# Decode attention over two caches: the TensorE program of the second part as a loop over chunk pairs, with fixed buffer pairs

## The chip, the cores and the metric

The kernel runs on one core of a Trainium2 chip. The metric is the device time of one execution in microseconds (us), as the median of several runs. The profiled span, from the first to the last instruction, is about 1.8 us shorter than the measured time.

TensorE is called PE here, and PEld is its weight load, which has its own row in the profile. DVE is VectorE, ACT is ScalarE, POOL is GpSimd, and SP is the engine that issues the large transfers. T, S and PV are the three matmul groups of a chunk: transposing K, scores, and probabilities times V.

## The reference

There are two attention layers with one query token each, whose outputs are concatenated. Layer A has 8 key/value heads for 32 query heads and sees only the last 2048 positions. Layer B has 32 heads and sees all 8192. The batch is 4 and the head size 128.

```python
# A: W = min(4096, max(256, Sk // 4)), only the last W positions, each kv head serves 4 query heads
# B: all Sk = 8192 positions, H = 32
q = (x @ wq).reshape(B, Sq, H, Dh).transpose(0, 2, 1, 3)
scores = jnp.einsum("bhqd,bhkd->bhqk", q, k_cache) * (Dh ** -0.5)
p = softmax(scores, axis=-1)
o = jnp.einsum("bhqk,bhkd->bhqd", p, v_cache)
out = o.transpose(0, 2, 1, 3).reshape(B, Sq, H * Dh) @ wo      # [...] concatenated: A, then B
```

The caches of B alone are 2 x 268 MB, so the kernel mostly reads memory.

## The kernel before

The work is cut into chunks: 8 of A (one key/value head, all batches, 2 MB of K and 2 MB of V) and 64 of B (two heads of one batch, 4 MB and 4 MB). K and V land in ten "halves" of 2 MB each, which are dealt out as a ring:

```python
def take(load, n, release, at=None):
    if at is None:
        if n == 2 and ring[0] % 2:
            ring[0] += 1
        at = ring[0] % NH            # NH = 10 halves; an A load takes one, a B load two
        ring[0] = at + n
    waits = []
    for i in range(at, at + n):
        waits += held[i]             # the last reader of the half: T for a K, PV for a V
        held[i] = [release]
    half_of[load] = at
    return at, waits
```

The loads go out on one queue in the order K(c+1), V(c), with the last four V at the end. A chunk has 16 groups of 8 tiles (8 in A). PE transposes a group of K (T), another engine copies it out of PSUM, and PE multiplies it with the query (S). After softmax, PE multiplies with V (PV). A table by group index mixes T, S and PV of several chunks, and the whole list is written out:

```python
for s in range(len(groups)):
    when(s, 0, lambda s=s: emit_T(s))
    when(s + SLAG, 2, lambda s=s: emit_S(s))
# [...] statistics
    v0 = max(s0 + PVLAG[ch["ab"]], v_end)            # PVLAG = {0: 6, 1: 8}
    for g in range(ch["NG"]):
        when(v0 + g, 4, lambda c=c, g=g: emit_pv(c, g))
# [...]
@block.tensor
def _(e):
    sch.emit("pe", e, sems)          # 26704 matmuls, each with its weight load, no loop
```

Of the kernel before, what the change touches and what calls it, by code (L numbers as in the profile page):

```python
# [12 lines left out]
P = 128  # L13
# [5 lines left out]
NPB = {0: 2, 1: 4}  # L19
NSM = 4  # L20
SLAG = 2
NW = 64
PVLAG = {0: 6, 1: 8}
# [5 lines left out]
class _Sched:  # L29


    def __init__(self):
        self.tk = {}
        self.ops = {n: [] for n in ("sp", "pe", "dve", "act", "pool")}
        self.count = {n: 0 for n in self.ops}
        self.dma_uses = {}

    def add(self, eng, emit, waits=(), key=None):
        sig = None
        if key is not None:  # L40
            self.count[eng] += 1
            sig = ("eng_" + eng, 1)
            assert key not in self.tk, key
            self.tk[key] = ("eng_" + eng, self.count[eng])
        self.ops[eng].append((emit, tuple(waits), sig))

    def add_dma(self, eng, emit, semname, waits=(), key=None):
        n = self.dma_uses.get(semname, 0) + 1
        self.dma_uses[semname] = n
        if key is not None:  # L50
            assert key not in self.tk, key
            self.tk[key] = (semname, 16 * n)
        self.ops[eng].append((emit, tuple(waits), (semname, 16)))

    def emit(self, engname, eng, sems):
        waited = {}
        for emit, waits, sig in self.ops[engname]:
            need = {}
            for w in waits:
                sname, val = self.tk[w]  # L60
                if need.get(sname, 0) < val:
                    need[sname] = val
            for sname, val in need.items():
                if waited.get(sname, 0) >= val:
                    continue
                eng.wait_ge(sems[sname], val)
                waited[sname] = val
            ins = emit(eng)
            if sig is not None:
                ins.then_inc(sems[sig[0]], sig[1])  # L70


def bass_concat_heads__sliding_block_cached__mha_block_cached__decode_kernel(
# [49 lines left out]

    sch = _Sched()
    with ExitStack() as es:
# [9 lines left out]
        kt = sb("kt", [P, NKT, TG * P], BF16)  # L135
        wor = sb("wor", [P, NWO, 4 * DO], BF16)
# [17 lines left out]
        rst = {0: sb("rsa", [P, NSM, 16], F32), 1: sb("rsb", [P, NSM, 2 * NB], F32)}  # L154
        rinv = sb("rinv", [P, NSM, 16], F32)
        pbt = {0: sb("pba", [P, NPB[0], NTA * 16 + NW], BF16), 1: sb("pbb", [P, NPB[1], NTB * 2 + NW], BF16)}
        oT = sb("oT", [P, NSM, 16], BF16)
        outsb = sb("outsb", [36, DO], BF16)
# [22 lines left out]
        sch.add("pool", lambda e: e.memset(rst[1][:, :, :], 0.0), key="c_rs")  # L181
# [6 lines left out]
        ring = [0]  # L188

        def take(load, n, release, at=None):  # L190
            if at is None:
                if n == 2 and ring[0] % 2:
                    ring[0] += 1
                at = ring[0] % NH
                ring[0] = at + n
# [5 lines left out]
            return at, waits  # L201
# [7 lines left out]
        def dma_wq(ab, at):  # L209

            at, waits = take(("wq", ab), 2, ("qmm", ab), at)
# [3 lines left out]
        def dma_wo(i):  # L215
# [4 lines left out]
            waits = [("fin", wo_last[i - NWO])] if i >= NWO else []  # L220
            sch.add_dma("sp", lambda e: e.dma_start(dst, src), "d_wo%d" % slot, waits=waits, key=("wo", i))

        def dma_kv(kind, c):
            ch = chunks[c]
            T = {("k", 0): A_k, ("k", 1): B_k, ("v", 0): A_v, ("v", 1): B_v}[(kind, ch["ab"])]
            at, waits = take((kind, c), 1 if ch["ab"] == 0 else 2, ("T", ch["s_last"]) if kind == "k" else ("pv", c))
# [18 lines left out]
        dma_wq(0, NH - 2)  # L245
        dma_kv("k", 0)
        dma_wq(1, NH - 4)

        loads = [("k", c + 1) for c in range(NC - 1)]
        for c in range(NC):  # L250
            loads.insert(2 * c + 1 if c < NC - 4 else len(loads), ("v", c))
# [12 lines left out]
        rs_read = [[] for _ in range(NSM)]  # L264


        def emit_xT():
            for ab in (0, 1):
                xv = xs[:, ab, :].rearrange("b (p r) -> b r p", r=KC)
                for r in range(KC):  # L270
                    o = xtps[:, (ab * KC + r) * NB:(ab * KC + r + 1) * NB]
                    i_ = xv[:, r, :]
                    sch.add("pe", lambda e, o=o, i_=i_: e.transpose(o, i_, identb[0:NB, 0:NB]),
                            waits=[("x", 0), ("x", 1), "c_identb"], key="xTmm" if (ab == 1 and r == KC - 1) else None)
# [4 lines left out]
        def emit_q(ab):  # L279
            wqr = flat(half_of[("wq", ab)], 2)  # L280
            for h in range(HQ):
                for r in range(KC):
                    o = ms[:, Q0 + h * NB: Q0 + (h + 1) * NB]
                    l = wqr[:, (r * HQ + h) * P:(r * HQ + h + 1) * P]
                    rr = xT[:, ab, r * NB:(r + 1) * NB]
                    last = h == HQ - 1 and r == KC - 1
                    sch.add("pe", lambda e, o=o, l=l, rr=rr, r=r: e.matmul(o, l, rr, start=(r == 0), stop=(r == KC - 1)),
                            waits=[("wq", ab), "xT"] + ms_read if h == r == 0 else [],
                            key=("qmm", ab) if last else None)
# [18 lines left out]

        def emit_T(s):
            c, g = groups[s]  # L310
            bank = s % NTRB
            for t in range(TG):
                o = tr[:, bank, t * P:(t + 1) * P]
                i_ = tile_of("k", c, g * TG + t)
                waits = []
                if t == 0:
                    waits = [("k", c), "c_identb"] + ([("ev", s - NTRB)] if s >= NTRB else [])
                sch.add("pe", lambda e, o=o, i_=i_: e.transpose(o, i_, identb[:, :]),  # L318
                        waits=waits, key=("T", s) if t == TG - 1 else None)
            src, dst = tr[:, bank, :], kt[:, s % NKT, :]  # L320
            waits = [("T", s)] + ([("S", s - NKT)] if s >= NKT else [])
            if s % 3 == 2 or (c < NCA and s % 2 == 1):
# [7 lines left out]

        def emit_S(s):
            c, g = groups[s]
            ch = chunks[c]
            for t in range(TG):
                j = g * TG + t
                if ch["ab"] == 1:
                    bank, o0, col = c % 2, 2 * j, NB * HQ + ch["b"] * HQ + 2 * ch["hp"]
                else:
                    bank, o0, col = j // HT, 16 * (j % HT), 16 * ch["g"]

                n = min(NW, 512 - o0)
                q = qs[:, col:col + n]
                o = sc[:, bank, o0:o0 + n]
                l = kt[:, s % NKT, t * P:(t + 1) * P]
                waits = []
                if t == 0:
                    waits = [("ev", s), ("q", ch["ab"])] + sc_read[bank]
                    sc_read[bank] = []
                sch.add("pe", lambda e, o=o, l=l, q=q: e.matmul(o, l, q, start=True, stop=True),  # L349
                        waits=waits, key=("S", s) if t == TG - 1 else None)  # L350
# [35 lines left out]
        def stats_gmax(c):  # L386
# [3 lines left out]
            sch.add("pe", lambda e: e.transpose(ms[0:C, col:col + P], rm[:, m, 0:C], identf[:, :]),  # L390
                    waits=[("rowmax", c), "c_identf"] + ms_read, key=("trm", c))
# [10 lines left out]
        def stats_exp(c):  # L402
# [3 lines left out]
            sch.add("pe", lambda e: e.matmul(ms[:, col:col + C], gx[0:C, m, :], identf[0:C, 0:C], start=True, stop=True),  # L406
                    waits=[("gx", c)] + ms_read, key=("bc", c))
            sch.add("dve", lambda e: e.tensor_copy(negb[:, m, 0:C], ms[:, col:col + C]), waits=[("bc", c)], key=("negb", c))  # L408
            ms_read[:] = [("negb", c)]
            i = c % NPB[ab]  # L410
            prev = c - NPB[ab]
            pw = [("c_pb", ab)] + ([("pv", prev)] if prev >= (0 if ab == 0 else NCA) else [])
            pbv = pbt[ab][:, i, 0:ch["NT"] * ch["UC"]].rearrange("p (j x) -> p j x", x=ch["UC"])
            r = ch["norm"] % NSM
            if ab == 1:
                for u, pp in HALVES:
                    src = sc[pp, c % 2, 0:NTB * 2].rearrange("p (j u) -> p u j", u=2)[:, u, :]
                    ri = rst[1][pp, r, ch["n0"] + u:ch["n0"] + u + 1]
                    sch.add("act", lambda e, src=src, pp=pp, ri=ri, u=u: e.activation(  # L419
                        pbv[pp, :, u], src, ACTF.Exp, bias=negb[pp, m, 0:1], scale=scale, accum_out=ri),  # L420
                        waits=[("negb", c), "c_rs"] + rs_read[r] + pw, key=("exp", c) if u == 1 else None)
# [14 lines left out]
            sch.add("dve", lambda e: e.tensor_reduce(out=rs4[:, r, :], in_=ev.rearrange("p (j c) -> p c j", c=C), axis=AX.X, op=ALU.add),  # L436
                    waits=[("exp1", c)], key=("rs4", c))
            sch.add("dve", lambda e: e.tensor_tensor(  # L438
                out=rst[0][:, r, :].rearrange("p (b c) -> p b c", b=NB), in0=bcast(rs4[:, r, :], [[0, NB], [1, C]]),
                in1=bcast(mk[:, :], [[1, NB], [0, C]]), op=ALU.mult),  # L440
                waits=[("rs4", c)] + rs_read[r], key=("rs", c))


        def emit_pv(c, g):
            ch = chunks[c]
            UC = ch["UC"]
            base = (ch["norm"] % NSM) * 16 + ch["n0"]
            for t in range(TG):
                j = g * TG + t
                n = NW if c < NC - 4 else UC  # L450
                o = po[:, base:base + n]
                l = tile_of("v", c, j)
                r = pbt[ch["ab"]][:, c % NPB[ch["ab"]], j * UC:j * UC + n]
# [3 lines left out]
                elif j == 0:  # L457
                    waits += [("v", c)]
                sch.add("pe", lambda e, o=o, l=l, r=r, j=j: e.matmul(o, l, r, start=(j == 0), stop=(j == ch["NT"] - 1)),  # L459
                        waits=waits, key=("pv", c) if j == ch["NT"] - 1 else None)  # L460

        def norm_n(c):
            return chunks[c]["norm"] % NSM, 16 if chunks[c]["ab"] == 0 else 2 * NB

        def norm_sum(c):
            m, n = norm_n(c)
            sch.add("pe", lambda e: e.matmul(ms[:, L0:L0 + n], onesf[:, :], rst[chunks[c]["ab"]][:, m, 0:n], start=True, stop=True),
                    waits=[("rs", c), "c_onesf"] + ms_read, key=("L", c))
            sch.add("dve", lambda e: e.reciprocal(out=rinv[:, m, 0:n], in_=ms[:, L0:L0 + n]), waits=[("L", c)], key=("rinv", c))
# [3 lines left out]
        def norm_out(c):  # L473
            m, n = norm_n(c)
            sch.add("dve", lambda e: e.tensor_tensor(out=oT[:, m, 0:n], in0=po[:, m * 16:m * 16 + n], in1=rinv[:, m, 0:n], op=ALU.mult),  # L475
                    waits=[("rinv", c), ("pv", c)], key=("oT", c))
            po_read[:] = [("oT", c)]

        def emit_fin(c):
            ch = chunks[c]  # L480
            ab = ch["ab"]
            m, n = norm_n(c)
            w = wor[:, ch["wo"] % NWO, :].rearrange("p (hl n) -> p hl n", hl=4)
            p0 = 0 if ab == 1 else 32
            if ab == 1:
                ov = oT[:, m, 0:n].rearrange("p (b u) -> p b u", u=2)
                ops = [(ov[:, :, u], w[:, (2 * ch["hp"] + u) % 4, :]) for u in range(2)]
            else:
                ov = oT[:, m, 0:n].rearrange("p (u c) -> p u c", c=REP)
# [100 lines left out]
```

## Time and profile before

| | before |
|---|---|
| time, median of 4 runs | 1419.8 us (1419.24 to 1420.34) |
| profiled span, granted PE clock | 1417.6 us, 0.958 |
| data queue q1 | 587.22 MB, 97.8% |
| instruction transfers of PE (fetches, queue q8) | 208, 1.0% |
| PE waits called "issue" (PE rows) | 41.4 + 33.8 + 33.4 = 108.6 us |

PE's rows of the waits say what PE lacks; the columns are total us, times, longest.

```profile
PE tr L318 <- DMA kv<-in_B_k_cache_dram: 96.5, 51, 4.5
PE po L459 <- issue: 41.4, 44, 2.4
PE sc L349 <- issue: 33.8, 32, 2.6
PE tr L318 <- issue: 33.4, 34, 2.2
```

PE lacks K for 96.5 us, and it lacks something that is no data for 108.6 us, in many short pieces.

### The profile page before, as it was taken

To read this page: it belongs to the slowest core of one execution; us is meant where nothing else is said; L and a number is where in the kernel's file an instruction comes from. 1 tells how busy PE (TensorE), PEld (TensorE's weight loads), DVE (VectorE), ACT (ScalarE), POOL (GpSimd) and SP (SyncE) were. 2 spreads that over 40 slices of the span, in tenths; PEclk is the share of its full clock that TensorE was granted. 3 is DMA by queue.
4 is the path that set the end of the run, shared out by engine and by line. 5 is a ranking of instruction groups with operands and counts; after the bars stand their busy time and mean duration, and the time that the engine had idled before them with its cause. 6 is when DMAs were issued, how large, how long until landed. Compare 5 with 4: busy or idle time off the path is not lost.

```text
span 1417.6 us, 55508 instructions
## 1 busy us (share of the span) xinstructions
PE 1148.0 (81%) x26704; PEld 1088.8 (77%) x26704; DVE 618.3 (44%) x1167; ACT 454.4 (32%) x649; POOL 19.6 (1%) x20
## 2 busy tenths in 40 slices
PE   4778888878888888887878888888787788888887
PEld 4667787778777778887778778877777788778786
DVE  1766443444444444444434444444344334434452
ACT  1443333323233333232333223333233233323331
POOL 1111000000000000000000000000000000000000
PEclk8999999999999999999999999999999999999997
DMA  9999999999999999999999999999999999999994
GB/s 400 414 417 422 429 426 429 429 426 430 427 427 426 426 427 432 416 424 429 411 429 426 419 404 431 417 426 415 418 428 427 423 412 416 429 422 408 423 426 206
DMA packets 30159, 590.76 MB, mean 417 GB/s; under 512 B 2656, under 2 KB 10864, under 8 KB 11120
## 3 DMA queue, kind: packets, MB, share of 16 engines
q1 hardware_dynamic: 29912, 587.22, 97.8%
q8 instruction: 208, 3.41, 1.0%
q14 instruction: 15, 0.12, 0.0%
q10 hardware_dynamic: 24, 0.01, 0.0%
HBM read 587.21 MB, written 0.01 MB: 414 GB/s over the span
## 4 chain that ended last, share of the span: by engine, by line
DMA 59%; PE 31%; DVE 6%; issue 3%; ACT 0%; SPq 0%; DVEq 0%
DMA kv<-in_B_k_cache_dram 57%; PE tr L318 14%; PE po L459 7%; PE sc L349 7%; DMA kv<-in_A_k_cache_dram 2%; DVE kt L325 2%; DVE sA L368 1%; PE ms L406 1%; DVE rsa L438 1%; PE fin L495 1%; DVE rm L383 1%; PE ms L390 1%; DVE sel L361 1%; DVE rm L378 0%; DVE rs L436 0%
## 5 line engine op out<-in xcount | busy, mean ns | idle before, releaser
L318 PE MATMUL tr<-identb,kv 128*128 128x128 bf16 x8704 | 690.7, 223 | 132.7 <-DMA kv<-in_B_k_cache_dram 96.5
L325 DVE COPY kt<-tr 128x1024 bf16<-128x1024 bf16 x704 | 486.6, 691 | 683.7 <-PE tr L318 680.8
L323 ACT ACTIVATE kt<-tr 128x1024 bf16<-128x1024 bf16 x384 | 392.3, 1024 | 854.8 <-PE tr L318 851.0
L318 PEld LDWEIGHTS tr<-identb,kv 128*128 128x128 bf16 x8704 | 520.0, 100 | 145.1 <-DMA kv<-in_B_k_cache_dram 103.0
L349 PE MATMUL sc<-qs,kt 128*128 128x64 bf16 x8704 | 449.8, 195 | 39.1 <-issue 33.8
L459 PE MATMUL po<-pbb,kv 128*128 128x64 bf16 (+1 forms) x8192 | 413.1, 192 | 43.5 <-issue 41.4
L349 PEld LDWEIGHTS sc<-qs,kt 128*128 128x128 bf16 x8704 | 373.2, 99 | 45.0 <-issue 35.9
L459 PEld LDWEIGHTS po<-pbb,kv 128*128 128x128 bf16 x8192 | 316.2, 99 | 56.8 <-issue 53.6
L419 ACT ACTIVATE pbb<-sc,negb 64x128 bf16<-64x128 f32 x128 | 51.5, 402 | 81.7 <-DVE negb L408 80.4
L383 DVE TENSOR_REDUCE rm<-sc 64x1 f32<-64x128 f32 x128 | 36.5, 285 | 18.5 <-PE sc L349 17.6
L390 PE MATMUL ms<-identf,rm 128*1 128x128 f32 (+1 forms) x72 | 21.0, 291 | 25.3 <-DVE rm L378 14.3
L390 PEld LDWEIGHTS ms<-identf,rm 128*1 128x1 f32 (+1 forms) x72 | 6.2, 86 | 35.1 <-DVE rm L383 19.2
L406 PEld LDWEIGHTS ms<-identf,gx 1*128 1x128 f32 (+1 forms) x144 | 21.1, 182 | 11.7 <-DVE gx L399 6.0
L406 PE MATMUL ms<-identf,gx 1*128 1x1 f32 (+1 forms) x144 | 27.2, 256 | 2.3 <-DVE gx L399 1.6
L459 PE MATMUL po<-pba,kv 128*128 128x64 bf16 x512 | 25.4, 193 | 0.0
L395 DVE TENSOR_REDUCE gm<-ms 1x2 f32<-1x128 f32 (+1 forms) x72 | 19.6, 272 | 11.6 <-PE ms L390 11.6
L495 PE MATMUL fin<-wor,oT 128*4 128x512 bf16 x64 | 18.3, 386 | 7.0 <-DVE oT L475 7.0
L419 ACT ACTIVATION_READ_ACCUMULATOR pbb<-sc,negb 64x1 f32 x128 | 23.7, 185 | 0.0
L459 PEld LDWEIGHTS po<-pba,kv 128*128 128x128 bf16 x512 | 19.1, 98 | 3.1 <-issue 3.1
L408 DVE COPY negb<-ms 128x1 f32<-128x1 f32 (+1 forms) x72 | 11.0, 152 | 15.4 <-PE ms L406 15.4
L368 DVE TENSOR_REDUCE sA<-sel 128x128 f32<-128x512 f32 x16 | 16.9, 1059 | 0.5
L399 DVE TENSOR_SCALAR gx<-gm 1x128 f32<-1x128 f32 (+1 forms) x72 | 15.9, 221 | 2.5
(36 smaller groups left out, 106.8 us busy)
## 6 DMA issues: line engine op xcount, KB each, us to landing
kv<-in_B_k_cache_dram SPq DMA_DIRECT2D x64, 4096.0 KB, 29.6
kv<-in_B_v_cache_dram SPq DMA_DIRECT2D x63, 4096.0 KB, 32.3
kv<-in_A_k_cache_dram SPq DMA_DIRECT2D x8, 2048.0 KB, 25.4
kv<-in_A_v_cache_dram SPq DMA_DIRECT2D x8, 2048.0 KB, 25.1
kv<-in_A_wq_dram SPq DMA_DIRECT2D x1, 4096.0 KB, 12.1
kv<-in_B_wq_dram SPq DMA_DIRECT2D x1, 4096.0 KB, 27.1
wor<-in_A_wo_dram SPq DMA_DIRECT2D x8, 512.0 KB, 16.3
wor<-in_B_wo_dram SPq DMA_DIRECT2D x8, 512.0 KB, 33.3
```

Source lines behind the costliest of these rows:

```text
L318: sch.add("pe", lambda e, o=o, i_=i_: e.transpose(o, i_, identb[:, :]), waits=waits, key=("T", s) if t == TG - 1 else None)
L323: sch.add("act", lambda e: e.activation(dst, src, ACTF.Copy), waits=waits, key=("ev", s))
L325: sch.add("dve", lambda e: e.tensor_copy(dst, src), waits=waits, key=("ev", s))
L349: sch.add("pe", lambda e, o=o, l=l, q=q: e.matmul(o, l, q, start=True, stop=True), waits=waits, key=("S", s) if t == TG - 1 else None)
L368: sch.add("dve", lambda e: e.tensor_reduce(out=dst, in_=sel[:, :].rearrange("p (j b c) -> p j c b", b=NB, c=REP), axis=AX.X, op=ALU.add), ...
L383: sch.add("dve", lambda e, src=src, pp=pp: e.tensor_reduce(out=rm[pp, m, 0:1], in_=src, axis=AX.X, op=ALU.max), waits=[("S", ch["s_last"]) ...
L390: sch.add("pe", lambda e: e.transpose(ms[0:C, col:col + P], rm[:, m, 0:C], identf[:, :]), waits=[("rowmax", c), "c_identf"] + ms_read, key ...
L395: sch.add("dve", lambda e: e.tensor_reduce(out=gm[0:C, m, 0:U], in_=src, axis=AX.X, op=ALU.max), waits=[("trm", c)], key=("gmax", c))
L406: sch.add("pe", lambda e: e.matmul(ms[:, col:col + C], gx[0:C, m, :], identf[0:C, 0:C], start=True, stop=True), waits=[("gx", c)] + ms_rea ...
L419: sch.add("act", lambda e, src=src, pp=pp, ri=ri, u=u: e.activation(pbv[pp, :, u], src, ACTF.Exp, bias=negb[pp, m, 0:1], scale=scale, accu ...
L459: sch.add("pe", lambda e, o=o, l=l, r=r, j=j: e.matmul(o, l, r, start=(j == 0), stop=(j == ch["NT"] - 1)), waits=waits, key=("pv", c) if j ...
L495: sch.add("pe", lambda e, l=l, r=r, st=st, sp_=sp_: e.matmul(fin[p0:p0 + NB, :], l, r, start=st, stop=sp_), waits=[("oT", c), ("wo", ch["w ...
```

## The change

The intent is that PE's program for B becomes a loop over pairs of chunks whose body is fetched once and not again in each turn (the kernel before: 208 transfers). For that, every turn must have the same instructions, buffers and semaphore steps. B gets two fixed K and two fixed V buffers of 4 MB in place of the ring. The query is copied to a fixed place (`qb`), the output weights too (`wos`), and PV of the chunk before is done as a block after T and S.

```diff
+        HALF_A = {"k": (3, 8, 0, 1, 2), "v": (7, 9, 4, 5, 6)}
-        def take(load, n, release, at=None):
-            if at is None:
-                [... ring ...]
+        def take(load, at, n, release):
[...]
-            at, waits = take((kind, c), 1 if ch["ab"] == 0 else 2, [...])
+            at = HALF_A[kind][c % 5] if ch["ab"] == 0 else (0 if kind == "k" else 4) + 2 * (c % 2)
+            waits = take((kind, c), at, 1 if ch["ab"] == 0 else 2, [...])
[...]
-            loads.insert(2 * c + 1 if c < NC - 4 else len(loads), ("v", c))
+            loads.insert(2 * c + 1, ("v", c))
[...]
-            if s % 3 == 2 or (c < NCA and s % 2 == 1):
+            if (g % 3 == 2) if c >= NCA else (g % 2 == 1):
                 sch.add("act", [... eviction on ACT, else on DVE ...])
[...]
+        def keys_part(c):
+            if c >= NCA and (c - NCA) % 2 == 0:
+                sch.mark()                          # the list may be repeated from mark to mark
+            for g in range(ch["NG"]):
+                emit_T(ch["s"] + g)
+                if g >= SLAG: emit_S(ch["s"] + g - SLAG)
+                [... statistics and output of earlier chunks ...]
+        def values_part(c, nxt):
+            [... PV of chunk c as a block, the last S and the statistics of nxt between ...]
+        for c in range(NC):
+            keys_part(c)
+            values_part(c - 1 if c else None, c)
[...]
+    def emit_looped(self, engname, eng, sems, loop):
+        a, b, steps = self.periods()                # longest run of equal stretches
+        [... pe and m: PE's list and its marks ...]
+        self.emit_ops(pe[:m[a]], eng, sems)
+        with loop(0, b - a) as i:
+            self.emit_ops(pe[m[a]:m[a + 1]], eng, sems, lambda sname, val: i * steps[sname] + val if steps[sname] else val)
+        self.emit_ops(pe[m[b]:], eng, sems)
[...]
-            sch.emit("pe", e, sems)
+            sch.emit_looped("pe", e, sems, loop)
```

Only PE has a loop. The other engines' programs stay written out.

## The prediction

> **What bounds the kernel now.** I read the busy slices first, then the DMA queues, then the waits, then the sixteen completion marks that the trace keeps for each transfer.
>
> ```profile
> DMA  9999999999999999999999999999999999999994
> q1 hardware_dynamic: 29912, 587.22, 97.8%
> q8 instruction: 208, 3.41, 1.0%
> DMA 59%; PE 31%; DVE 6%; issue 3%; ACT 0%; SPq 0%; DVEq 0%
> ```
>
> The sixteen DMA engines are busy from end to end; 587 MB has to come in whatever the program looks like. Beside it 208 instruction transfers take 1.0%. The chain of the page agrees: mostly the K loads. So PE time by itself is worth little, and what counts is what the data stream loses, when it starts to run dry, and how long the work is after its last byte.
>
> ```profile
> PEld tr L318 <- DMA kv<-in_B_k_cache_dram: 103.0, 53, 4.6
> PEld po L459 <- issue: 56.6, 65, 2.7
> PEld tr L318 <- issue: 39.2, 39, 2.4
> PEld sc L349 <- issue: 35.9, 34, 2.2
> ```
>
> In the waits PE stands 103 us for K data and 131.7 us (56.6 + 39.2 + 35.9) for "issue": nothing the profile shows, in pieces up to 2.7 us. I take these for PE waiting for its own instructions: counting PE instructions at the start of each q8 transfer, each starts just after PE has crossed another multiple of 256.
>
> The 1.0% understates the fetches. In the trace a 32 KB piece takes 1213 ns on one engine, and a 4 MB transfer (8 pieces on each engine) takes 9.71 us. At 12.7 to 12.9 us, before the first fetch, all sixteen engines finish a transfer together. Then eight fall behind and eight do not: the K load issued at 131 us has eight marks by 154.1 and the other eight at 156.1 to 157.9; at 449 us 466.6 to 469.7 against 479.1 to 480.9; the last piece of V 1391.3 to 1393.7 against 1407.0 to 1409.1. The slow marks differ among themselves by steps of some 1.6 us. So the fetches go through eight engines, and a transfer is only done when the slowest has finished. The fast engines keep 9.71 us per transfer until their queue runs dry from about 700 us on. Extended without gaps, their line (marks at 230.5 and 563.7 us: 34 transfers and two of 1.5 us for wo) ends at 1367.7 us. The real end is 1409.1: the fetches cost 41.4 us, or 0.20 us each, four times what 1.0% suggests.
>
> [...]2 x 26704 instructions / 256 = 208.6, and 3.41 MB / 208 = 16.4 KB.[...]
>
> **The change, part by part.**
>
> *Loop.* The instruction order of the changed kernel has 3275 matmuls ahead of the loop, 775 in the body (one pair of chunks), 906 behind. With two instructions each and 46 register and wait instructions, the body is 1596: seven blocks of 256[...].[...] The loop runs 29 times (32 pairs less two before and one after). Fetches: 26 + 7 + 7 = 40 in place of 208 if the body stays. Straight gain: 168 x 0.20 = 34 us. The loop's own cost, some 40 register instructions and a branch per 39 us, lies beside the data.
>
> *Order of PE.* T and S of a chunk first, then PV of the chunk before as a block. In dense stretches 8 T take 0.42 us, 8 S 0.26, 8 PV 0.23, so a B chunk takes 16 x 0.91 = 14.6 us and about 1 for statistics. The data of one chunk takes 19.4. PE has 3 to 4 us of slack[...].
>
> *Fixed buffers.* B now has two K and two V buffers of 4 MB where the ring had five. Counting from the landing of K(c+1) at L: K(c+3) is issued when its T ends, about L+12, V(c+2) about L+17, while the queue still holds V(c), K(c+2), V(c+1), until L+29. Steady state never runs dry.
>
> *The seam from A to B.* Here it costs. The first B load of K goes into halves 0 and 1; half 0 holds the last A chunk's K, so it must wait for that chunk's transposes. Before, the ring had free halves:
>
> ```profile
> 96.29 0.37 SPq L221 DMA_DIRECT2D wor<-in_A_wo_dram  x1
> 96.70 0.51 SPq L241 DMA_DIRECT2D kv<-in_B_k_cache_dram  x1
> 97.25 0.55 SPq L229 DMA_DIRECT2D kv<-in_A_v_cache_dram  x1
> 109.46 0.37 SPq L221 DMA_DIRECT2D wor<-in_A_wo_dram  x1
> 109.87 1.58 SPq L241 DMA_DIRECT2D kv<-in_B_k_cache_dram  x1
> ```
>
> This timeline of the DMA queue shows the first B load issued at 96.7, before the loads ahead of it were through (109.6). When does the last A chunk's T end now? The A stage is slower than its data, and DVE sets its pace:
>
> ```profile
> L368 DVE TENSOR_REDUCE sA<-sel 128x128 f32<-128x512 f32 x10 | 10.6, 1058 | 0.3
> L325 DVE COPY kt<-tr 128x1024 bf16<-128x1024 bf16 x12 | 8.2, 683 | 3.8 <-PE tr L318 3.8
> L438 DVE TENSOR_TENSOR rsa<-rs,mk 128x16 f32<-128x16 f32 x5 | 7.6, 1514 | 0.2
> L361 DVE TENSOR_TENSOR sel<-sc,mk 128x512 f32<-128x512 f32 x10 | 6.6, 657 | 7.3 <-PE sc L349 7.3
> ```
>
> These groups of DVE from 60 to 120 us, about five chunks, belong to a cycle of 12.8 us (mean spacing of the maximum's transposes). The change gives DVE four evictions a chunk instead of 2.7 (the rule was every third group to ScalarE as well as odd ones). Its sum per chunk: 4 x 0.68 + 2 x (0.66 + 1.06) + 1.51 + 0.60 + 0.43 + 0.42 + 0.54 + 0.16 + 0.25 + 0.17 = 10.2 us, and about 3 us of waits for matmuls in the two statistics chains: 13.3 us. From the second chunk's keys at 34 us (15 us for that cold first one), the last chunk starts at about 49 + 5 x 13.3 = 115.5 and its T end 7 us later: 122 us. The queue is empty at 109.6; the first B load lands 11.9 us after issue (9.7 of data and 2.2 of start, as the first load of all). It lands at 134 where the fast line has 115.9: 18 us lost.
>
> A second gap follows: the first B V waits for PV of the last A chunk, which now stands behind all T and S of the first B chunk, about 134 + 16 + 2.5 = 152.6. The data issued meanwhile ends at 150, and a start costs 2.2: 5 us lost.
>
> *The end.* Before, V of the last four chunks came last and their PV ran with a cold clock and fetch stalls:
>
> ```profile
> 1380.00:1400.00 20.00, 15.76 (x384) 14.69 (x384) 9.06 (x20) 5.92 (x12) 0.00 (x0) 0.91 0.76 320
> 1400.00:1417.00 17.00, 11.98 (x382) 10.82 (x382) 1.05 (x3) 0.00 (x0) 0.00 (x0) 0.50 0.24 96
> ```
>
> In this table by stage (PE, PEld, DVE, ACT, POOL, clock, DMA share, GB/s) the last 17 us run at half clock with PE alone; 8.5 us lie behind the last landing. Now one PV block is left, behind a PV of the chunk before: about 3.5 us and the same 3.8 of output. I keep 7.5.
>
> *Sum.* Fast line 1367.7, seam +18 (all engines are level again there), second gap +5, fetches after it (9 + 7 + 7) x 0.20 = +4.6: data ends at 1395. Plus 7.5, plus 2 between span and measured time (1419.6 against 1417.6): 1404.8. I round the guesses down a little, to 1403.
>
> **The rivals.** (1) The body doesn't stay in PE's memory[...]. Then 7 x 29 fetches come back with a stall at each back edge, the eight engines lag as before, the seam is paid on top: about 1403 + 196 x 0.20 = 1442.[...] I give it 1 in 10. (2) The seam is cheap: DVE keeps 12.6 us a chunk and the second gap closes. Then 7 to 9 us come back: about 1395; below 1392 the change would be over 2% faster. (3) PE or the two buffers become the bound in the steady state, because T and S now crowd the evictions: a group every 0.68 us against 0.69 (DVE, two of three) and 1.02 (ACT): DVE needs 0.46 per group, so it should hold. If not, each us over 19.6 a chunk costs 64 us; I give it 1 in 30.
>
> **Range and chances.** The seam (plus or minus 6 us) and the end (3) set the inner range, 1393 to 1412; the first rival's tail widens it above. Over 2% faster needs a seam nearly free: 0.09. Over 2% slower needs more than rival 1 alone: 0.05.
>
> **What would show it.** Right: about 40 instruction transfers, a q8 share near 0.2%; landings of all engines within about 5 us at the end; "issue" waits of PE mostly gone, its waits for K grown past 200 us; DMA slices full but for a dip around 110 to 125 us (and perhaps 150); first B K issued near 122 us. Wrong: over 200 instruction transfers; no dip; K and V waits short with PE over 90% busy.

Cut from it, where marked, is what no run of this case shows: how much PE's instruction memory holds and how far ahead it is fetched, how the DMA engines share their time, and an allowance for the clock that had no working. No term of the sum is among the cuts; it came to 1404.8 us, rounded to 1403.

Three of its readings of the trace need their numbers. The k-th fetch starts when PE has begun between 43 fewer and 193 more than 256 k matmuls and weight loads, at the median 111 more; each of the 208 is of 16384 bytes. The fast engines' marks, 9.7 to 9.8 us apart for 4 MB, first come later at 583.5 us (10.1 behind the one before), not from about 700. And the profile doesn't name the engine of a fetch: that each falls on one engine, and all of PE's on eight, is read from the marks. In the changed kernel PE fetches once between 255.6 and 1363.8 us, at 294.6. With this fetch one of the sixteen marks goes from 3.8 to 5.2 us behind the first (transfers with first marks at 287.8 and 297.5), another goes from 1.3 to 2.3 with a transfer of queue 14 at 298.3, and until 386 us, with no fetch, all lags stay the same within 0.1 us.

## More of the kernel before

One view is added here because the changed kernel looks different in it: the table by stage of the kernel before, around the passage from A to B. Columns are the window, its length, busy time and instructions of PE, PEld, DVE, ACT and POOL, then the granted PE clock, the DMA share and GB/s.

```profile
98.90:111.00 12.10, 8.43 (x179) 7.31 (x180) 7.77 (x14) 5.21 (x7) 1.89 (x1) 1.00 1.04 428
111.00:118.00 7.00, 5.18 (x125) 4.88 (x123) 5.47 (x10) 3.07 (x5) 1.47 (x1) 1.00 0.98 419
118.00:133.00 15.00, 11.40 (x242) 9.69 (x240) 11.50 (x22) 5.84 (x7) 2.31 (x2) 1.00 1.03 428
133.00:150.00 17.00, 15.63 (x332) 13.77 (x331) 8.88 (x18) 5.57 (x9) 0.00 (x0) 1.00 1.01 419
```

The data stream passes from A to B without a gap: the DMA share is about 1 in every row.

## The result, and the profile after

The changed kernel takes 1403.94 us (1403.74 to 1404.69, 4 runs) against 1419.8 us. The ratio is 0.9889 (95% interval 0.9872 to 0.9906). A ratio is the mean time of one kernel's fast runs over that of the other's of the same rounds, so it is not quite the quotient of the medians. That is 1.1% faster, which counts as the same at the threshold of 2%. All results are correct.

These are lines of the page of the changed kernel: the span, busy time of the engines, the DMA slices and GB/s over the span, the queues, and the chain that ended last.

```profile
span 1402.8 us, 57072 instructions
PE 1175.2 (84%) x26768; PEld 1133.0 (81%) x26768; DVE 673.4 (48%) x1327; ACT 423.3 (30%) x617; POOL 19.2 (1%) x22
DMA  9997899999999999999999999999999999999995
GB/s 400 416 413 286 357 429 428 432 432 425 431 430 433 430 433 430 431 428 434 432 431 430 428 432 433 434 427 430 432 431 433 429 430 433 433 426 435 431 431 251
q1 hardware_dynamic: 29912, 587.22, 98.0%
q8 instruction: 40, 0.66, 0.2%
q14 instruction: 16, 0.13, 0.0%
DMA 62%; PE 33%; DVE 4%; issue 1%; ACT 0%; SPq 0%; ACTq 0%; DVEq 0%
```

The fetches fell from 208 to 40. The DMA slices, all 9 but the last before, now have a dip in the fourth and fifth: the data stream stops there. The waits of the changed kernel:

```profile
PE tr L320 <- DMA kv<-in_B_k_cache_dram: 168.5, 57, 10.4
PEld tr L320 <- issue: 110.9, 67, 6.0
...
PE po L322 <- issue: 12.3, 8, 2.6
...
PE tr L320 <- issue: 6.2, 2, 5.9
```

PE's own "issue" rows are down from 108.6 to 18.5 us, and its wait for K grew from 96.5 to 168.5 us. The second line is a trap. Inside the loop PE waits on a semaphore against a register's value. Of its 110.9 us of "issue" on the weight load, 83.9 lie inside the pauses that the first line already counts as waits for K on the matmul (overlap of the two rows' pauses in the trace). Its longest pause, 6.0 us at 213.3 us, is the entry to the loop; PE's own row shows it as 5.9.

The timeline of the DMA queue and the table by stage show the dip (columns as for the kernel before):

```profile
89.82 0.37 SPq L268 DMA_DIRECT2D wor<-in_A_wo_dram  x1
117.18 0.35 SPq L290 DMA_DIRECT2D kv<-in_B_k_cache_dram  x1
117.57 0.55 SPq L278 DMA_DIRECT2D kv<-in_A_v_cache_dram  x1
118.16 0.59 SPq L268 DMA_DIRECT2D wor<-in_A_wo_dram  x1
118.80 0.63 SPq L290 DMA_DIRECT2D kv<-in_B_k_cache_dram  x1
148.63 0.34 SPq L290 DMA_DIRECT2D kv<-in_B_v_cache_dram  x1
```

```profile
98.90:111.00 12.10, 9.65 (x207) 8.29 (x203) 9.69 (x18) 4.51 (x5) 1.89 (x1) 1.00 0.66 268
111.00:118.00 7.00, 6.19 (x119) 5.09 (x114) 5.90 (x11) 3.28 (x4) 1.89 (x1) 1.00 0.01 2
118.00:133.00 15.00, 4.30 (x82) 4.10 (x80) 4.19 (x9) 0.21 (x1) 0.00 (x0) 0.64 0.99 406
133.00:150.00 17.00, 15.46 (x311) 14.05 (x309) 10.86 (x23) 5.54 (x6) 1.89 (x1) 0.91 0.79 315
```

Nothing is issued between 89.8 and 117.2 us, and from 111 to 118 us next to nothing moves (2 GB/s). The first load of B waits for half 0, which the last A chunk's K still holds. A second, smaller hole follows: the first V of B is issued only at 148.6 us.

The sixteen completion marks of each transfer (one for each DMA engine, read from the trace in order of time) show how the end is composed. The last piece of V, marks in us:

```
before     1391.3 1391.3 1391.4 1391.8 1392.0 1392.2 1392.7 1393.7 1407.0 1407.1 1408.4 1408.5 1408.6 1408.6 1408.6 1409.1
after      1386.6 1386.6 1386.7 1386.8 1386.9 1387.2 1389.6 1389.8 1390.0 1390.1 1391.3 1391.4 1391.4 1391.6 1391.6 1395.4
dvedouble  1396.0 1396.0 1396.0 1396.1 1396.1 1396.1 1396.1 1396.2 1396.2 1396.2 1396.2 1396.2 1396.2 1396.3 1397.5 1404.0
```

(The third row is an experiment below.) Before, half the engines came 15 us late. After, they are within 5 us, except one straggler at 1395.4, which alone sets the end of the data. From it to the end of the span are 7.4 us. That is a distance, and not work that waited for this landing: PE's timeline shows that PE last waited for the last K and never for the last V.

```profile
1375.89 2.74 PE L320 MATMUL tr<-identb,kv 128*128 128x128 bf16 x24 [1.55 <-DMA kv<-in_B_k_cache_dram]
...
1395.42 0.39 PE L322 MATMUL ms<-rsb,onesf 128*128 128x4 f32 x2 [0.86 <-ACT pbb L481]
1395.66 3.36 PE L322 MATMUL po<-pbb,kv 128*128 128x2 bf16 x128
```

The last K landed at 1375.8, again with one straggler (the fifteenth mark is at 1372.2). From there PE works for 27 us to the end, and the last PV starts when the exponentials are done.

### The profile page after: what moved, and what is told of

The parts are those of the page before. It is cut to its first block, busy times and chain, and to the rows that moved or that the text cites. A ratio compares the mean times of both kernels' runs of the same rounds, so it can differ in the third digit from the quotient of the medians.

```text
span 1402.8 us, 57072 instructions
## 1 busy us (share of the span) xinstructions
PE 1175.2 (84%) x26768; PEld 1133.0 (81%) x26768; DVE 673.4 (48%) x1327; ACT 423.3 (30%) x617; POOL 19.2 (1%) x22
## 4 chain that ended last, share of the span: by engine, by line
DMA 62%; PE 33%; DVE 4%; issue 1%; ACT 0%; SPq 0%; ACTq 0%; DVEq 0%
DMA kv<-in_B_k_cache_dram 59%; PE tr L320 20%; PE sc L322 9%; PE po L322 2%; DMA kv<-in_A_k_cache_dram 1%; PE fin L322 1%; DMA kv<-in_A_wq_dram 1%; DVE kt L383 1%; DVE rsa L500 1%; DVE sA L432 1%; PE ms L322 1%; DVE sel L425 1%; DVE rm L442 0%; DVE sA L489 0%; DVE rs L498 0%
## 5 line engine op out<-in xcount | busy, mean ns | idle before, releaser
L320 PE MATMUL tr<-identb,kv 128*128 128x128 bf16 x8704 | 705.1, 232 | 176.6 <-DMA kv<-in_B_k_cache_dram 168.5
L383 DVE COPY kt<-tr 128x1024 bf16<-128x1024 bf16 x736 | 502.8, 691 | 491.8 <-PE tr L320 487.5
L320 PEld LDWEIGHTS tr<-identb,kv 128*128 128x128 bf16 x8704 | 560.2, 105 | 203.2 <-issue 110.9
L381 ACT ACTIVATE kt<-tr 128x1024 bf16<-128x1024 bf16 x352 | 360.5, 1024 | 668.7 <-PE tr L320 666.1
L322 PE MATMUL sc<-qb,kt 128*128 128x64 bf16 x8192 | 424.7, 197 | 0.9 <-DVE kt L383 0.7
L322 PEld LDWEIGHTS sc<-qb,kt 128*128 128x128 bf16 x8192 | 351.4, 101 | 2.8 <-DVE kt L383 0.9
L322 PE MATMUL po<-pbb,kv 128*128 128x64 bf16 (+1 forms) x8192 | 290.1, 191 | 12.5 <-issue 12.3
L322 PEld LDWEIGHTS po<-pbb,kv 128*128 128x128 bf16 x8192 | 263.0, 97 | 13.2 <-issue 11.1
L322 PE MATMUL sc<-qs,kt 128*128 128x64 bf16 (+3 forms) x512 | 26.3, 197 | 16.5 <-DVE kt L383 16.5
L322 PEld LDWEIGHTS sc<-qs,kt 128*128 128x128 bf16 x512 | 21.2, 101 | 19.6 <-DVE kt L383 19.4
L322 PE MATMUL fin<-wos,oz 128*4 128x512 bf16 x64 | 19.6, 388 | 0.3 <-DVE oz L541 0.3
L320 PE MATMUL ms<-identf,rm 128*1 128x128 f32 (+1 forms) x72 | 19.6, 273 | 0.2 <-DVE rm L447 0.2
```

The source lines that it names most:

```text
L320: emit = lambda e: e.transpose(o, l, r)
L322: emit = lambda e: e.matmul(o, l, r, start=start, stop=stop)
L381: sch.add("act", lambda e: e.activation(dst, src, ACTF.Copy), waits=waits, key=("ev", s))
L383: sch.add("dve", lambda e: e.tensor_copy(dst, src), waits=waits, key=("ev", s))
```

## The experiments

Nine kernels ran, in three calls; each call has its own runs of the kernel before as the base. All gave correct results.

### unrolled: the changed kernel without the loop

```diff
-            sch.emit_looped("pe", e, sems, loop)
+            sch.emit("pe", e, sems)
```

> The changed kernel with PE's program written out in full: same order, same buffers, no loop. My theory: some 209 instruction transfers in place of 40, each costing 0.20 us at the end of the data because the fetches go through eight of the sixteen DMA engines: 169 x 0.20 = 34 us, so about 1437 us (1430 to 1444), with the slow eight engines again some 12 us or more behind the fast eight. Rival A, fetches cost only their 1.0% share of DMA time: about 1415. Rival B, the gain came from the new order and not from the loop: 1404, no change.

Measured: 1434.8 us (1432.3 to 1436.61), ratio 1.0105 (1.0088 to 1.0122). Its queue line and waits:

```profile
q8 instruction: 209, 3.42, 0.9%
```

```profile
PE po L322 <- issue: 114.3, 61, 3.3
...
PE tr L320 <- DMA kv<-in_B_k_cache_dram: 56.5, 25, 10.7
...
PE sc L322 <- issue: 25.3, 31, 2.0
...
PE tr L320 <- issue: 11.1, 14, 1.7
```

The loop alone is worth 1434.8 - 1403.9 = 30.9 us, for 169 fetches: 0.18 us each, where the prediction had 0.20. The fetch waits are back on PE (114.3 + 25.3 + 11.1 = 150.7 us), and from 780 us to the last K the slowest DMA engine is 13 to 18 us behind the fastest again (8.5 to 13.4 between the two halves). Without the loop, the other parts of the change cost 15 us.

A rival has to be ruled out here: that PE's own stalls, and not the slow DMA engines, made the time. The page's chain even suggests it:

```profile
PE 53%; DMA 34%; issue 8%; DVE 4%; ACT 0%; SPq 0%; ACTq 0%; DVEq 0%
```

The trace speaks against it. Between 200 and 1380 us every load was issued at least 13.7 us before the slowest engine had finished the load ahead of it (16.8 in the kernel before), so PE never let the slow engines run dry. The data ends at 1424.3 us against 1395.4, which is 28.9 of the 31.0 us between the spans (0.17 us for each fetch). The other 2.1 us come behind it (9.5 against 7.4).

### seamfix and kfix: other places for two of A's buffers

Half 0 must be free when the first K of B is due, and half 4 when its first V is. In HALF_A the last A chunk's K sits in half 0, and its V in 4. The change swaps each with the neighbour that is released one chunk earlier. The table serves chunks 1 and 2 as well, so their places swap too. That moved little: the last load ahead of the seam goes out at 90.0 us instead of 89.8.

```diff
-        HALF_A = {"k": (3, 8, 0, 1, 2), "v": (7, 9, 4, 5, 6)}
+        HALF_A = {"k": (3, 0, 8, 1, 2), "v": (7, 4, 9, 5, 6)}     # seamfix; kfix: only "k"
```

> The changed kernel with another choice of halves for the A chunks, so that the last A chunk's K and V lie in halves 8 and 9, which B never uses. My theory: the first B K load waits for the T of the last chunk but one (about 105 us in place of 117.2) and the first B V for that chunk's PV, both before the queue is empty; the two gaps (about 13 and 6 us) close, and the engines keep a lag of some 3 us that the gaps had levelled: 1387 us (1384 to 1391). Rival, the gaps only move the waiting (PE is then the bound, or a later buffer stalls): 1398 or more.

> As before, but only the K halves are moved; V of the last A chunk stays in half 4. My theory: the first gap closes (13 us), the second, at the first B V, stays and grows a little because the data ahead of it is through earlier: about 8 us lost in place of 19, so about 1393 us (1389 to 1398). Rival, the two gaps are one and the same: then either all is gained (1387) or nothing (1404).

Measured: seamfix 1388.26 us (1387.82 to 1389.02), ratio 0.9782 (0.9765 to 0.9798). kfix 1393.2 us (1392.38 to 1393.26), ratio 0.9814 (0.9797 to 0.983), which leaves open whether it is 2% faster. DMA slices and timeline of the DMA queue of seamfix:

```profile
DMA  9999999999999999999999999999999999999996
```

```profile
90.02 0.37 SPq L268 DMA_DIRECT2D wor<-in_A_wo_dram  x1
105.27 0.35 SPq L290 DMA_DIRECT2D kv<-in_B_k_cache_dram  x1
...
120.43 0.34 SPq L290 DMA_DIRECT2D kv<-in_B_v_cache_dram  x1
```

The first K of B goes out at 105.3 instead of 117.2, its V at 120.4 instead of 148.6, and the dip is gone. Of the 15.7 us, K brings 1403.9 - 1393.2 = 10.7 and V 4.9. In kfix V was still issued only at 137.28. This seamfix version is 2.2% faster than the kernel before. It gains 15.7 us and not the 18.5 that the fast engines lost at the seam. At equal transfers the slowest engine is 15.2 us earlier than in the changed kernel, from 190 us on, and stays 15.1 to 15.9 us earlier to the end. Of the difference, 1.1 us is still lost at the seam (first K at 117.0, where the kernel before has 115.9). The rest went with the pause itself: in the changed kernel it let the engines draw level (marks of the first K of B at 128.8 to 129.3, one at 130.5), in seamfix they stay apart (117.0 to 119.7).

### seamunrolled: the same seam, without the loop

```diff
-        HALF_A = {"k": (3, 8, 0, 1, 2), "v": (7, 9, 4, 5, 6)}
+        HALF_A = {"k": (3, 0, 8, 1, 2), "v": (7, 4, 9, 5, 6)}
-            sch.emit_looped("pe", e, sems, loop)
+            sch.emit("pe", e, sems)
```

> The version without the gaps at the seam (1388 us), with PE's program written out in full. It has the change's order of PE and its fixed buffers, but neither its loop nor its gaps. My theory: the loop is worth some 31 us here too, as between 1404 and 1435, and the new order by itself nothing, so 1419 us (1414 to 1425), the time of the kernel before. Rival, the order in blocks and the fixed buffers help or harm by themselves: 1410 or less, or 1430 or more.

Measured: 1419.71 us (1417.67 to 1423.46), ratio 0.9999 (0.9982 to 1.0017). With the seam mended and no loop, the new order and the fixed buffers together are worth nothing against the kernel before. The loop is worth 1419.7 - 1388.3 = 31.4 us here, as much as with the gaps at the seam: the two effects add.

### dvedouble: twice the instruction transfers of DVE

In the loop of the changed kernel one engine of sixteen still falls back, in steps of about 0.9 us, and each step coincides with an instruction transfer of queue 14 (8 KB each). The trace does not name the engine that it is for. These come every 135 to 140 us; two others of the queue, at 968.7 and 1248.8 us, fall close to them, but 841.2 and 1115.6 stand alone. That they are DVE's is what the experiment tests. From the trace, in us:

```
transfer on queue 14 starts           841.2   980.8   1115.6  1251.4
first mark of a transfer at     799.1  847.7   994.9   1142.1  1289.2
its last mark behind its first   5.1    5.9     6.9      7.8     8.8
```

The experiment adds 1024 tiny copies to DVE, which is little work and many instructions.

```diff
+        scr = sb("scr", [P, 1024], BF16)
[...]
+            if c >= NCA:
+                sch.add("dve", lambda e: e.tensor_copy(scr[:, 16 * (c - NCA) + g:16 * (c - NCA) + g + 1], mkb[:, 0:1]), waits=["mkb"])
```

> The changed kernel with 1024 tiny copies added on DVE, one per group of the B part: DVE's program grows by some 1024 instructions, eight more instruction transfers of 8 KB on queue 14. My theory, formed from the trace after: in the loop one single DMA engine falls back by some 0.9 us at each such transfer (8.9 us at the end against 5 of the others), and the data ends with it: +7 us, about 1411 (1408 to 1414). Rival, that engine is slow for another cause: 1404 to 1405, and its lag at the end still about 9 us.

Measured: 1411.6 us (1410.58 to 1412.15), ratio 0.9943 (0.9926 to 0.996), as expected. The queue line:

```profile
q14 instruction: 24, 0.20, 0.0%
```

It has 8 more transfers (24 against 16) with 1024 more instructions of DVE, and takes 7.7 us more. The marks above show where the time goes: the straggler is at 1404.0, the others at 1396.0 to 1397.5. DVE's busy time grew too (673.4 to 723.7 us), but fourteen engines are within 0.3 us of each other at the end, so the single late one is what a DVE that was merely slower would not explain.

### body13: a loop body of four chunks

Marks every four chunks give a body of about 3190 instructions, twelve and a half blocks where the changed kernel's has seven, in 14 turns. How much PE keeps is not known from the runs before. If it is less than this body, everything is fetched again.

```diff
-            if c >= NCA and (c - NCA) % 2 == 0:
+            if c >= NCA and (c - NCA) % 4 == 0:
                 sch.mark()
```

> The changed kernel with a loop body of two pairs of chunks: about 3190 instructions, 12.5 blocks of 256[...]. My theory: every block is fetched again in each of the 14 turns, some 220 instruction transfers, and the time goes back to that of the written-out program, about 1440 us (1432 to 1450), with PE stalls at the back edges hidden in its slack. Rival, a loop as such spares the fetches whatever its size: about 40 to 50 transfers and 1404 us.

Measured: 1510.67 us (1507.2 to 1513.91), ratio 1.0651 (1.0625 to 1.0676). The fetches came back as expected; the size of the loss was missed by 70 us. Queue, chain and PE's waits of body13:

```profile
q8 instruction: 234, 3.83, 1.0%
PE 71%; issue 17%; DMA 6%; DVE 5%; ACT 0%; SPq 0%; ACTq 0%; DVEq 0%
```

```profile
PE po L322 <- issue: 118.3, 51, 3.8
...
PE tr L320 <- issue: 98.7, 32, 7.3
...
PE sc L322 <- issue: 36.8, 34, 2.1
...
PE tr L320 <- DMA kv<-in_B_k_cache_dram: 17.3, 3, 10.3
```

PE is the bound now; it hardly ever waits for K (17.3 us). Against the unrolled kernel its "issue" rows are 253.8 - 150.7 = 103.1 us longer. At the 13 back edges alone stand 79.6 us, 5.2 to 7.5 each (from the start of the last matmul to the start of the next). Of these the K waits absorb 56.5 - 17.3 = 39.2, and PE's busy time grows by 1190.3 - 1176.8 = 13.5. The balance is 103.1 - 39.2 + 13.5 = 77 us, and the spans differ by 1506.8 - 1433.8 = 73.0. The expected 1440 would have needed these stalls to fit into PE's waits for data, and the unrolled kernel had only 56.5 us of those, beside fetch stalls that stay. Here PE does let the DMA engines run dry: 10 of 116 loads between 200 and 1380 us were issued only after even the slowest engine had finished the load ahead, where the unrolled kernel has none.

### body13hint: the same, with a hint for the back edge

```diff
-                return nc.Fori([...], head_slot={pe: 0})
+                return nc.Fori([...], head_slot={pe: 0}, hint_back_edge=True)
```

> The loop with a body of two pairs (1511 us, 234 instruction transfers), with a hint at the top of each turn[...]. My theory: of its 107 us over the one-pair loop some 75 are the stalls of 5 to 7.5 us at 14 back edges[...], in a phase in which PE has no slack left; with the hint they shrink to the ordinary stalls and the time falls to that of the written-out program, 1440 us (1428 to 1455), with still over 200 transfers. Rival, the excess is not the back edge but the fetches within the body: 1495 or more.

Measured: 1505.23 us (1498.75 to 1509.27), ratio 1.06 (1.0571 to 1.063), with 222 fetches. The theory behind the 1440 falls: the hint shortened the gaps at the back edges only from 79.6 to 60.3 us in all (3.5 to 5.6 each). It stays open why 19 us less of gaps moved the time by 5.5 us only.

### tailorder: the new end in the old kernel

The kernel before holds back the last four V and their PV. This takes that out of it and changes nothing else.

```diff
-            loads.insert(2 * c + 1 if c < NC - 4 else len(loads), ("v", c))
+            loads.insert(2 * c + 1, ("v", c))
[...]
-                n = NW if c < NC - 4 else UC
+                n = NW if c < NC - 1 else UC
[...]
-            if c == NC - 4:
-                v0 = max(v0, chunks[NC - 1]["s_last"] + 1)
```

> The kernel before with the last four V loads in their ordinary place, so that the last PV do not all stand behind the last landing, as the change has it. My theory: the end of the data is set by the slow engines and stays at about 1409 us; behind it 7.5 us in place of 8.5, so 1417 to 1421, the same time. Rival, the long tail of PV at half clock was a large part of the change's gain: 1412 or less.

Measured: 1421.01 us (1420.6 to 1421.5), ratio 1.0014 (0.9997 to 1.0031). The last landing is 1408.9 against 1409.1 us. Behind it stand 10.6 us, where 7.5 had been expected and the kernel before has 8.5. The order at the end was worth nothing in the old kernel. That this is so because the slow engines set the last landing is argued, not tested.

### best: seamfix with a rearranged end

The last K is loaded one place earlier, T and S of the last two chunks stand ahead of the last three PV, and the last V has its own halves.

```diff
[... HALF_A as in seamfix ...]
+            if kind == "v" and c == NC - 1:
+                at = 8
[...]
+        i = loads.index(("k", NC - 1))
+        loads[i - 1], loads[i] = loads[i], loads[i - 1]
[...]
-        for c in range(NC):
+        for c in range(NC - 2):
             [...]
+        for c in (NC - 2, NC - 1):
+            [... keys_part and the last S ...]
+        for c in (NC - 3, NC - 2):
+            [... PV in blocks, statistics of the last chunk between ...]
[... changes to where the last chunk's statistics stand in keys_part ...]
```

> The version without the gaps (1388 us), with the end rearranged: the last K is loaded one place earlier, its T and S run ahead of the last three PV, and the last V lies in halves 8 and 9, so that its load waits for nothing. My theory: behind the last landing only some 16 tiles of PV and the output stay, 4 to 5 us in place of 7.4, so 1385 us (1383 to 1388). Rival, the end is not PE's chain after the last K, or the pulled-up K delays the V loads: 1388 or more.

Measured: 1386.56 us (1385.74 to 1390.25, 5 runs), ratio 0.977 (0.9756 to 0.9783). The time behind the last landing shrank from 7.2 us (seamfix) to 5.5, and the landing stayed (1379.3 against 1379.4). In both kernels PE does not wait for that landing: its last PV begins without a wait for data. The gain of 1.7 us, of 3 expected, is not resolved: its interval overlaps with seamfix's, and the two ran on different chips. Both beat the kernel before and the changed one.

## Why the prediction was right or wrong

The total was right, 1403 against 1403.94 us, and so was the mechanism of the loop and of the seam. Two terms of the sum were mis-sized by nearly the same amount in opposite directions, so the hit is partly luck.

- **Loop.** Right: 40 fetches predicted, 40 in the trace. 25 come before the loop, 7 in its first turn, one at 294.6 us in the third, none from there to 1363.8 us, and 7 behind the loop. The gain of 34 us measured 30.9 (31.4 with the seam mended). The mis-sized term is the cost of one fetch, 0.18 instead of 0.20 us. Two readings on the way there were wrong: 41.4 us are not "four times" but about three times what 1.0% of the span suggests (14.2 us), and "PE stands 103 us" and 131.7 are rows of the weight load, where PE's own are 96.5 and 108.6. Rival 1, that the body doesn't stay, fell; body13 shows a body that doesn't stay (234 fetches). The runs show that a body of seven blocks is not fetched again and one of twelve and a half is; where between them the limit lies was not tested. body13 is 107 us slower than the changed kernel with half as many turns, where the rival had been given 39 us.
- **First gap.** The mechanism was right (half 0 held by the last A chunk), the size was not: "18 us lost" measured 12.9 (first B K at 128.8 against 115.9 on the fast engines). The failing term is the cycle of A, "13.3 us". It measured about 12.15: in the window of one cycle DVE is busy 9.69 of 12.10 us where the sum had 10.2, and what remains for waits is 2.4 where I had put 3. Two smaller errors nearly cancel: the cycles began at 47.3 us and not at 49, and the last chunk's T took 9.0 us and not 7. So the first load went out at 117.2, not 122. Once issued it took 11.6 us to land (11.9 predicted).
- **Second gap.** "5 us lost" measured 5.6: between the second K and the first V of B lie 160.2 - 144.9 = 15.3 us, where the kernel before has 9.7. kfix and seamfix set the worth of both gaps in time: 10.7 and 4.9 us.
- **Fetches after the seam.** "(9 + 7 + 7) x 0.20 = +4.6" measured 5.0 for the ordinary slow engines (1391.6 against 1386.6), but 8.8 for one. The step that failed is what was left out: I counted only PE's fetches on queue 8. DVE's fetches on queue 14, which the page shows with 0.0%, delay one engine by 0.9 us each. dvedouble shows that they set the end of the data.
- **End of the data.** 1367.7 + 12.9 + 5.6 + 8.8 = 1395.0, and 0.4 that I can't place, give the measured 1395.4. Predicted was 1395: the seam was 4.5 us cheaper than thought and the straggler 4.2 dearer.
- **The end.** The number was right, 7.5 us predicted and 7.4 measured, but the path was not: PE did not wait for the last V, as the sum has it. It waited for the last K, 27 us before the end, and the last PV began at 1395.7 because the work in between took that long. That this work, 19.9 us from the last K's landing to the last PV, equals the 19.6 us until the last V lands is luck. tailorder adds that the order of the last loads had not cost the old kernel anything.
- **Steady state.** Right: two buffers suffice. In the four stretches that I read between 300 and 1380 us the DMA share of the changed kernel is 1.00 to 1.01, at a granted clock of 0.92 to 0.94. Between 200 and 1370 us every load was issued at least 6.5 us before even the fastest engine had finished the one ahead. The trace shows a granted clock of 0.64 from 118 to 133 us, the stretch with PE's longest wait for K (10.4 us). seamunrolled, equal to the kernel before, shows that order and buffers as a whole neither help nor hurt.
- **The signs.** The dip, the queue share and the vanished "issue" waits came as named. The waits for K "past 200 us" did not: they are 168.5. "Landings within about 5 us" held for fifteen engines, not for the one that mattered.
- **What the prediction overlooked.** It took the seam as the price of fixed buffers. It was a free choice of two numbers in a table. Without the seam the change would have been 2.2% faster than before, outside the range of the prediction.

## What to carry to other kernels

When the data stream is the bound, look at when each DMA engine finishes a transfer, not at the queue's share. Here a queue with 1.0% went with eight engines that ended 15 us after the others, and one with 0.0% with a single engine that fell back by 0.9 us at a time. A loop whose body was not fetched again (40 transfers in place of 209) was 30.9 us faster than no loop, and one whose body was (234) was 75.9 us slower than no loop. When buffers become fixed, check each stage's first load against the last reader of its place.
